# Batch 1's inverse stage in units of three y tiles, the ordering copies ahead of hswish, and one first-stage copy on VectorE

## The chip, the cores and the metric

The kernel runs on one core of a Trainium2 chip. The metric is device time in microseconds (us) of one execution. The engines are named as in the profile: PE (TensorE: matmuls, its weight loads in a row of their own, PEld), DVE (VectorE), ACT (ScalarE), POOL (GpSimd) and SP (SyncE, here only a queue that issues DMAs).

## What is computed

```python
def _attn_ref(x, filt_r, filt_i):            # x: (8, 3008, 256), filt: (1505, 256)
    X = np.fft.rfft(x, axis=1)
    Y = X * (filt_r + 1j * filt_i)[None]
    return np.fft.irfft(Y, n=x.shape[1], axis=1)

def _moe_ref(x, w_in, w_out):                # x: (24064, 256), w_in: (256, 2048), w_out: (2048, 256)
    h = x @ w_in
    g = h * np.clip(h + 3.0, 0.0, 6.0) / 6.0
    return g @ w_out
```

The second function takes the first one's output, all eight batches as 24064 tokens. All is in float32.

## The kernel before

**The second part sets the pace.** The 24064 tokens are 47 blocks of 512, and the 2048 hidden columns are 8 parts of 256. The loop at line 1190 goes through items i = 8k + p (block k, part p); one pass is called *step i* here. A step computes the up products of (k, p) and the down products of the item before it. Both are done with seven products in place of eight, so that there are sums to make around them: `t_sums` on POOL (line 760, per block), `g_sums` and `g_last` on DVE (821, 822, 827, per step). In a step PE does, in this order: `up_1` (three products of line 764), the work of *place 0*, `down` 1 (line 843), `up_2`, `down` 2 and 4, `up_3`, `down` 5 and 6, the work of *place 1*, `up_5`, `down` 7 and 3. What the vector side does for it:

- ACT copies products out of PSUM (775, 776, 785, 804) and computes two relus (809, called relu 0 and relu 1).
- DVE makes two sums from PSUM (790, 795) and two hswish products (814). hswish 0 is issued at line 1246 after relu 0; hswish 1 is issued at the head of the next step, in `g_sums`, and `down` 2 and 4 need it.
- At the first part of a block the last block's output is finished: `out_4` (918, 919) reads the PSUM bank that `down` 5 opens again, `out_5` (923) another; at the last part `out_1` (900), `out_2` (909) and `out_3` (914).

**The first part is threaded into these steps.** For each batch b from 1 on: a first stage (`a_unit` for batch 1, `a6_unit` for the others), a store to DRAM and a load back, a second stage (`b_unit`), the filter (`f_unit`, three DVE instructions 560 to 562, then `y_unit`, two DVE instructions 571 and 572, per y tile), an inverse stage, and a store to `g_tmp`, from where `t4_load` and `n_five`/`n_unit` (704, 715) take it, some steps later, and write `xn`. There are 12 y tiles per batch. The inverse stage is `bi_unit` for batches 0 and 1, two y tiles per unit, and `bi3_unit` for batches 2 to 7, three y tiles per unit.

- `bi_unit` (line 583): eight matmul passes into two PSUM banks of the pool psF, then two ACT copies (586); its store is two DMAs on the POOL queue (630).
- `bi3_unit` (line 599): 24 passes in three rounds, into two psF banks and the bank `be`. The bank `be` is written in round one and in round three, from different rows of PE. Between them stands the *ordering copy* (601): DVE copies two columns of `be` as soon as round one has written them, and round three waits for that. Then ACT copies one bank (602), DVE the rest of `be` (603, called the third copy), and ACT the other bank after relu 1 (610, in `bi3_copies`). Its store is four DMAs on the POOL queue (615, 618). `a6_unit` has the same ordering copy (483).

**What sets the order.** Everything is in program order on each engine. A table, `plan`, says in which step and place a unit is issued: place 0 for `a_unit`, `b_unit`, `bi_unit`, `n_five`, `n_unit`; place 1 for `w_scale`, `bi3_unit`, `a6_unit`; place 2, at the end of the step, for the rest (stores, loads, sums, `f_unit`, `y_unit`). `places(1)` gives the steps of batch 1: `a_unit` in steps 2 to 9, `b_unit` and `f_unit` in 12, 13, 15, 18, 19, 20, 22, 23, 26, 27, 28, 30, `y_unit` in 14, 15, 16, 19, 21, 22, 24, 25, 27, 29, 30, 31, `bi_unit` in 16, 21, 24, 29, 31, 32. For batches 2 to 7 `bi3_unit` falls on steps with p = 3 and p = 1, in turn. `late` (line 1186) moves `g_last` within a step, by p and by what the step before held. psF has two banks, the pools of `be` and of the tile t that a unit stores have one buffer each.

In place 0 of step 8 (block 1, p = 0) `a_unit` does chunk c = 6 of batch 1: ACT copies its first bank (456), and `a_sums` in place 2 lets DVE copy the second (464).

Of the kernel before, what the change touches and what calls it, by code (L numbers as in the profile page):

```python
# [12 lines left out]
AXT = mybir.ActivationFunctionType  # L13
# [26 lines left out]
NB = HC // XC  # L40
# [142 lines left out]
def kernel(  # L183
# [9 lines left out]
    nc = tc.nc  # L193
# [54 lines left out]
    st = {}  # L248
# [161 lines left out]
    def copy(dve, to, ps):  # L410
        if dve:
            nc.vector.tensor_copy(out=to, in_=ps)
        else:
            nc.scalar.activation(out=to, in_=ps, func=AXT.Copy)
# [22 lines left out]
    def bank(b):  # L437
        if b:
            return psF.tile([P, 512], FP32, name="psf", tag="f")
        st["bank"] = i = (st.get("bank", -1) + 1) % 4  # L440
        return psO.tile([P, 2, 2, P], FP32, name="po%d" % i).rearrange("p a u m -> p (a u m)")
# [4 lines left out]
    def a_unit(b, c):  # L446
        xc = xs[:, (b * NB + c) % 3, :, :]
        t = t1p.tile([P, XC // 2, 2, D], FP32, name="t1")
        ps = [bank(b).rearrange("p (j d) -> p j d", d=D) for h in range(2)]
        for j in range(2):  # L450
            for g in range(2):
                for h in range(2):
                    nc.tensor.matmul(ps[h][ts(g, 64), j, :], wa[ds(h * 64, NA), ds((c * XC + 2 * g + j) * 2 * KH, 64)],
                                     xc[ds(h * 64, NA), 2 * g + j, :], start=True, stop=True)
        for h in range(2 if b == 1 and c < NB - 2 else 1):
            nc.scalar.activation(out=t[:, :, h, :], in_=ps[h], func=AXT.Copy)
        st["t1", b, c] = t, ps[1]


# [129 lines left out]
    def bi3_unit(b, i):  # L589
        ys = [st.pop(("y", b, i + v)) for v in range(3)]  # L590
        c = psU.tile([P, 512], FP32, name="be")
        banks = [psF.tile([P, 512], FP32, name="psf", tag="f") for ri in range(2)]
        t = t3p.tile([P, 3, 2, D], FP32, name="t3")
        to = [t[:, q, :, :].rearrange("p u d -> p (u d)") for q in range(3)]
        for r in range(3):
            for v in range(2):
                for ri in range(2):
                    x, u, ps, o = (2, v, c, ri) if r == 2 * ri else (v, r - 1 + ri, banks[ri], r - 1 + ri)
                    nc.tensor.matmul(ps[ts(v, 64), ts(o, D)], wi[ts(ri, 64), 0, :], ys[x][ts(ri, 64), u, :], start=True, stop=True)  # L599
            if r == 0:  # L600
                nc.vector.tensor_copy(out=to[2][:, 0:2], in_=c[:, 0:2])
        nc.scalar.activation(out=to[1], in_=banks[1], func=AXT.Copy)
        nc.vector.tensor_copy(out=to[2][:, 2:512], in_=c[:, 2:512])
        st["t3", b, i] = t
        st["bi3"] = to[0], banks[0]

    def bi3_copies():
        if "bi3" in st:
            to, ps = st.pop("bi3")
            nc.scalar.activation(out=to, in_=ps, func=AXT.Copy)  # L610

    def g3_store(b, i):
        t = st.pop(("t3", b, i))
# [22 lines left out]
    for b in range(B):  # L636
# [4 lines left out]
        n = 0  # L641
# [170 lines left out]
    def hswish(k, p, i):  # L812
        o = (G11, G12)[i]
        nc.vector.scalar_tensor_tensor(out=st["g", k, p][:, o:o + 2, :].rearrange("p a n -> p (a n)"),  # L814
                                       in0=st["r", i], scalar=1.0, in1=st["h"][i], op0=ALU.min, op1=ALU.mult)
# [159 lines left out]
    def at(step, fn, *a):  # L975
        plan.setdefault((step, 0 if fn in EARLY else 1 if fn in (w_scale, bi3_unit, a6_unit) else 2), []).append((fn, a))

    with tc.manual_schedule():
# [43 lines left out]
        ps = psU.tile([P, 512], FP32, name="al")  # L1022
# [117 lines left out]
        def places(n):  # L1140
            if n == 1:
                return (list(range(2, NB + 2)), [12, 13, 15, 18, 19, 20, 22, 23, 26, 27, 28, 30],
                        [14, 15, 16, 19, 21, 22, 24, 25, 27, 29, 30, 31], [16, 21, 24, 29, 31, 32])
            k = first[n] * NP
            a_at = [k - 7 * NP + i for i in A_AT]
            f_at, y_at, bi_at = ([k - (5 - 2 * r) * NP + i for r in range(2) for i in p]
                                 for p in ((2, 3, 6, 7, 12, 13), (4, 5, 10, 11, 14, 15), (11, 17)))
            return a_at, f_at, y_at, bi_at
# [4 lines left out]
        for n in range(1, B):  # L1153
            a_at, f_at, y_at, bi_at = places(n)
            for c, s in enumerate(a_at):
                at(s, a_unit if n == 1 else a6_unit, n, c)
                at(s, a_sums if n == 1 else a6_sums, n, c)
                at(s, *((z_store, n, c, nc.sync) if n == 1 else (z6_store, n, c)))
                if c >= (3 if n == 1 else 2):
                    at(max(a_at[c - 3 + (n > 1)], s - 6), x_load, n, c)  # L1160
                elif n > 1:
                    at(max(prev[-1 if n == 2 else c - 2], s - 6), x_load, n, c)
            for c in range(NT):
                s = f_at[2 * (c - TB) + (n == 1)] + 1 if c >= TB else a_at[-1] + 1
                at(s, t2_load, n, c)
                s = f_at[2 * (c - FB) + 1] + 1 if c >= FB else a_at[-1 if n > 1 else 3] + 1
                at(s, table_load, n, c)
            for i in range(NU):
                if i % 2 == 0 or n == 1:
                    at(f_at[i], b_unit, n, i)  # L1170
                if n == 1 and i % 2 == 0:
                    at(bi_at[i // 2], bi_unit, n, i)
                    at(bi_at[i // 2], g_store, n, i)
                if n > 1 and i % 3 == 0:
                    at(bi_at[i // 3], bi3_unit, n, i)
                    at(bi_at[i // 3], g3_store, n, i)
                at(y_at[i], y_unit, n, i)
            for i in range(NU):
                at(f_at[i], f_unit, n, i)
            prev = a_at  # L1180

        HEAVY = (f_unit, y_unit, a_sums, n_five, a6_sums, bi3_unit)

        def late(i):
            return i % NP in (1, 2) or any(fn in HEAVY for place in range(3) for fn, a in plan.get((i - 1, place), ()))

        items = [(k, p) for k in range(NBLK) for p in range(NP)]
        for i in range(len(items) + 1):  # L1190
            up = i < len(items)
            k, p = items[min(i, len(items) - 1)]
            dn = i > 0
            kd, pd = items[i - 1]
            def do(place):
                for fn, a in plan.get((i, place), ()):
                    fn(*a)

            if k == 0:
                plain_up(p)  # L1200
                do(0)
                if dn:
                    plain_down(pd)
                do(1)
                do(2)
                continue
            if not up:
                last_down()
                break
            up_1(k, p)  # L1210
            ends = k == LAST and p == NP - 1
            do(0)
            last_plain = dn and kd == 0
            dn = dn and kd > 0
            if dn:
                g_sums(kd, pd)
                if not late(i):
                    g_last(kd, pd)
                down(kd, pd, 1)
            if up:  # L1220
                up_2(k, p)
            if dn and pd == 0 and kd > 1:
                out_4(kd - 1)
            if up:
                up_2b(k, p)
            if dn:
                down(kd, pd, 2, 4)
                if pd == NP - 1:
                    out_1(kd)
            if up:  # L1230
                up_3(k, p)
                if dn and late(i) and not (pd == 0 and kd > 1):
                    g_last(kd, pd)
            if dn:
                down(kd, pd, 5, 6)
            if up:
                up_4(k, p)
            if ends:
                out_1(k)
            if last_plain:  # L1240
                plain_down(pd, (0,))
            if dn and pd == 0 and kd > 1:
                out_5(kd - 1)
                g_last(kd, pd)
            if up:
                hswish(k, p, 0)
                do(1)
            if up:
                up_5(k, p)
            bi3_copies()  # L1250
            if last_plain:
                plain_down(pd, (1,))
                plain_out()
            if dn:
                if pd == NP - 1 or ends:
                    out_2(kd)
                down(kd, pd, 7, 3)
                if pd == NP - 1 or ends:
                    out_3(kd)
            do(2)  # L1260
# [30 lines left out]
```

## Time and profile before

Three runs of the kernel took 2650.63, 2651.26 and 2653.53 us, median 2651.26 us. The profiled execution took 2651.27 us, of which its span, from the first to the last instruction, is 2649.5 us.

| | busy us | share of the span |
|---|---|---|
| PE matmul | 2634.2 | 99% |
| PE weight load | 2338.2 | 88% |
| DVE | 2045.6 | 77% |
| ACT | 1299.8 | 49% |
| POOL | 484.2 | 18% |

The mean granted clock of PE is 1.00 from step 8 on. The timeline of the weight loads shows each step: its first load of line 764 from `xn` into `be` marks the start, and the next one of that kind the end. Times "at 2.17" below count from there. The lengths of steps by what else they hold (starts in the timeline subtracted from each other):

| step holds | steps | length, us |
|---|---|---|
| nothing more | 208 | 6.15 (one 6.98) |
| `b_unit` of batch 1 | 12 | 7.01; in 20, 23, 28: 7.36; in 26: 7.64 |
| `n_five` | 32 | 7.66 to 7.75 |
| one `n_unit` (four matmul passes) | 3 | 6.60 |
| `a6_unit` of three tiles | 18 | 7.88 |
| the same and `n_five` | 12 | 9.39 |
| `bi_unit` of batch 1, steps 16, 21, 24, 29, 31, 32 | 6 | 8.91, 7.69, 7.69, 7.70, 8.91, 7.37 |
| `bi3_unit`, p = 3 | 9 | 7.86 |
| `bi3_unit`, p = 3, and one `n_unit` (steps 267, 315) | 2 | 8.61 |
| `bi3_unit`, p = 3, and `n_five` (step 299) | 1 | 10.08 |
| `bi3_unit`, p = 1, steps 81, 129, 177, 225, 257, 273, 321 | 7 | 7.96 |
| `bi3_unit`, p = 1, steps 65, 113, 161, 209, 305 | 5 | 8.29 to 8.30 |

In a plain step (34, from 320.17 us) the loads of `down` 2 and 4 begin at 2.17, those of `down` 5 and 6 at 3.50, and DVE's hswish 0 ends at 5.27.

### The profile page before, as it was taken

To read this page: it belongs to the slowest core of one execution; us is meant where nothing else is said; L and a number is where in the kernel's file an instruction comes from. 1 tells how busy PE (TensorE), PEld (TensorE's weight loads), DVE (VectorE), ACT (ScalarE), POOL (GpSimd) and SP (SyncE) were. 2 spreads that over 40 slices of the span, in tenths; PEclk is the share of its full clock that TensorE was granted. 3 is DMA by queue.
4 is the path that set the end of the run, shared out by engine and by line. 5 is a ranking of instruction groups with operands and counts; after the bars stand their busy time and mean duration, and the time that the engine had idled before them with its cause. 6 is when DMAs were issued, how large, how long until landed. Compare 5 with 4: busy or idle time off the path is not lost.

```text
span 2649.5 us, 54856 instructions
## 1 busy us (share of the span) xinstructions
PE 2634.2 (99%) x21872; PEld 2338.2 (88%) x21872; DVE 2045.6 (77%) x3602; ACT 1299.8 (49%) x2682; POOL 484.2 (18%) x707
## 2 busy tenths in 40 slices
PE   9999999999999999999999999999999999999999
PEld 6688888989889898898988988889888888999998
DVE  7878767887678876788767887688877878766666
ACT  4554444444545445454444544545445454454554
POOL 2242022121211202111021210211112120111110
PEclk9999999999999999999999999999999999999999
DMA  9732234112241133411233112331223321110000
GB/s 245 222 94 70 71 84 116 54 32 81 77 119 52 32 84 80 113 52 36 81 86 107 52 37 80 89 103 52 55 61 89 103 56 48 48 43 22 19 21 25
DMA packets 130646, 198.29 MB, mean 75 GB/s; under 512 B 21538, under 2 KB 97408, under 8 KB 130198
## 3 DMA queue, kind: packets, MB, share of 16 engines
q1 hardware_dynamic: 115165, 150.12, 20.8%
q0 software_dynamic: 14656, 44.16, 6.0%
q8 instruction: 173, 2.83, 0.4%
q14 instruction: 83, 0.68, 0.1%
q10 hardware_dynamic: 569, 0.50, 0.1%
HBM read 122.43 MB, written 83.98 MB: 78 GB/s over the span
## 4 chain that ended last, share of the span: by engine, by line
PE 96%; DMA 2%; DVE 2%; issue 0%; SPq 0%; ACT 0%; POOL 0%; POOLq 0%; DVEq 0%
PE po L843 43%; PE al L764 24%; PE be L764 18%; PE psn L704 2%; PE psf L539 1%; PE psf L480 1%; PE po L886 1%; PE be L599 1%; PE psf L599 1%; PE psf L583 1%; PE be L480 1%; DVE g L814 0%; PE al L875 0%; PE be L875 0%; DMA ft<-in_filt_i_dram 0%; PE po L548 0%
## 5 line engine op out<-in xcount | busy, mean ns | idle before, releaser
L843 PEld LDWEIGHTS po<-w_all,g 128*128 128x128 f32 x10276 | 1369.6, 191 | 112.5 <-issue 20.3
L843 PE MATMUL po<-w_all,g 128*128 128x128 f32 x10276 | 1395.0, 276 | 1.1 <-DVE g L814 0.9
L809 ACT ACTIVATE r<-h,half_c 128x512 f32<-128x512 f32 x736 | 531.0, 721 | 336.0 <-DVE h L790 324.0
L764 PE MATMUL al<-xt,w_all 128*128 128x256 f32 x2208 | 659.6, 381 | 0.1
L814 DVE SCALAR_TENSOR_TENSOR g<-r,h 128x512 f32<-128x512 f32 x736 | 534.1, 727 | 151.9 <-ACT r L809 135.8
L764 PE MATMUL be<-xt,w_all 128*128 128x256 f32 x1472 | 437.8, 379 | 0.0
L790 DVE TENSOR_TENSOR h<-be,s 128x512 f32<-128x512 f32 x368 | 253.6, 689 | 153.0 <-PE be L764 144.5
L764 PEld LDWEIGHTS al<-xt,w_all 128*128 128x128 f32 x2208 | 335.4, 192 | 1.0 <-issue 0.5
L764 PEld LDWEIGHTS be<-xt,w_all 128*128 128x128 f32 x1472 | 279.7, 190 | 37.9
L760 POOL TENSOR_TENSOR xt<-xn 128x256 f32<-128x256 f32 x184 | 142.7, 795 | 874.1 <-ACT xn L686 840.3
L804 ACT ACTIVATE h<-al 128x256 f32<-128x256 f32 x368 | 141.4, 384 | 298.4 <-PE al L764 298.4
L795 DVE TENSOR_TENSOR h<-al,s 128x256 f32<-128x256 f32 x368 | 156.0, 424 | 156.7 <-PE al L764 156.1
L822 DVE TENSOR_TENSOR g<-g 128x512 f32<-128x512 f32 x367 | 261.3, 712 | 12.6
L785 ACT ACTIVATE s<-al 128x256 f32<-128x256 f32 x368 | 141.4, 384 | 212.1 <-PE al L764 210.6
L764 PE MATMUL al<-xn,w_all 128*128 128x256 f32 x736 | 226.0, 389 | 0.0
L776 ACT ACTIVATE s<-be 128x256 f32<-128x256 f32 x368 | 141.4, 384 | 171.7 <-PE be L764 171.7
L764 PE MATMUL be<-xn,w_all 128*128 128x256 f32 x736 | 218.9, 379 | 0.0
L821 DVE TENSOR_TENSOR g<-g 128x256 f32<-128x256 f32 x367 | 167.1, 455 | 12.6
L775 ACT ACTIVATE s<-al 128x256 f32<-128x256 f32 x368 | 141.2, 384 | 65.5 <-PE al L764 65.5
L827 DVE TENSOR_TENSOR g<-g 128x256 f32<-128x256 f32 x367 | 160.1, 436 | 2.5
L764 PEld LDWEIGHTS be<-xn,w_all 128*128 128x128 f32 x736 | 139.8, 190 | 18.9
L920 POOL TENSOR_TENSOR o<-p,o 128x256 f32<-128x256 f32 x46 | 36.7, 799 | 602.4 <-DVE o L918 557.1
(171 smaller groups left out, 1927.8 us busy)
## 6 DMA issues: line engine op xcount, KB each, us to landing
t<-g_tmp SPq DMA_DIRECT2D x184, 120.0 KB
t<-z_tmp SPq DMA_DIRECT2D x42, 512.0 KB
g_tmp<-t POOLq DMA_DIRECT2D x72, 256.0 KB, 5.7
z_tmp<-t POOLq DMA_DIRECT2D x120, 144.0 KB, 3.4
o_tmp<-o SPq DMA_DIRECT2D x46, 256.0 KB
xs<-in_x_dram SPq DMA_DIRECT2D x60, 192.0 KB
ft<-in_filt_r_dram SPq DMA_DIRECT2D x168, 64.0 KB
ft<-in_filt_i_dram SPq DMA_DIRECT2D x168, 64.0 KB
```

Source lines behind the costliest of these rows:

```text
L760: nc.gpsimd.tensor_tensor(out=o, in0=x0, in1=x1, op=op_)
L764: nc.tensor.matmul(ps, w_in[p][:, w, :], x, start=start, stop=stop, skip_group_check=True)
L776: nc.scalar.activation(out=s5, in_=be[:, 1, :], func=AXT.Copy)
L785: nc.scalar.activation(out=s[:, 1, :], in_=al, func=AXT.Copy)
L790: nc.vector.tensor_tensor(out=st["h"][0].rearrange("p (a n) -> p a n", a=2), in0=be, in1=s, op=ALU.add)
L795: nc.vector.tensor_tensor(out=st["h"][1][:, 256:512], in0=al, in1=s5, op=ALU.add)
L809: nc.scalar.activation(out=r, in_=st["h"][i], func=AXT.Relu, bias=half_c, scale=1.0 / 6.0)
L814: nc.vector.scalar_tensor_tensor(out=st["g", k, p][:, o:o + 2, :].rearrange("p a n -> p (a n)"), in0=st["r", i], scalar=1.0, in1=st["h"][i ...
L821: v.tensor_tensor(out=g[:, G1, :], in0=g[:, G3, :], in1=g[:, G22, :], op=ALU.add)
L822: v.tensor_tensor(out=g[:, G3:G2 + 1:2, :], in0=g[:, G3:G1 + 1, :], in1=g[:, G11:G11 + 1, :].broadcast_to([P, 2, 256]), op=ALU.subtract)
L827: nc.vector.tensor_tensor(out=g[:, G4, :], in0=g[:, G12, :], in1=g[:, G2, :], op=ALU.subtract)
L843: nc.tensor.matmul(st["po", k][bank][:, part, u, :], g[:, a, ts(u, P)], w_out[p][:, w, :], start=(p == 0 and n in OPENS and u == 0), stop= ...
```

## The change

- Batch 1's inverse stage is issued as four `bi3_unit`s with `g3_store`, in place 1 of steps 17, 24, 29 and 32, instead of six `bi_unit`s with `g_store` in place 0 of steps 16, 21, 24, 29, 31 and 32. The y tile of step 25 is issued in step 24.
- Place 1 of a step comes ahead of hswish 0, so that on DVE the ordering copies (601, 483) stand before it. The third copy (603) goes to `bi3_copies`, and so stays behind hswish 0 on DVE. ACT's and PE's orders are not touched by this part.
- In `a_unit`, chunk c = 6 of batch 1 (step 8): the first bank's copy is DVE's instead of ACT's.

```diff
@@ a_unit
         for h in range(2 if b == 1 and c < NB - 2 else 1):
-            nc.scalar.activation(out=t[:, :, h, :], in_=ps[h], func=AXT.Copy)
+            copy(c == NB - 2, t[:, :, h, :], ps[h])
@@ bi3_unit
         nc.scalar.activation(out=to[1], in_=banks[1], func=AXT.Copy)
-        nc.vector.tensor_copy(out=to[2][:, 2:512], in_=c[:, 2:512])
         st["t3", b, i] = t
-        st["bi3"] = to[0], banks[0]
+        st["bi3"] = to[0], banks[0], to[2], c
 
     def bi3_copies():
         if "bi3" in st:
-            to, ps = st.pop("bi3")
+            to, ps, third, c = st.pop("bi3")
             nc.scalar.activation(out=to, in_=ps, func=AXT.Copy)
+            nc.vector.tensor_copy(out=third[:, 2:512], in_=c[:, 2:512])
@@ places
             if n == 1:
                 return (list(range(2, NB + 2)), [12, 13, 15, 18, 19, 20, 22, 23, 26, 27, 28, 30],
-                        [14, 15, 16, 19, 21, 22, 24, 25, 27, 29, 30, 31], [16, 21, 24, 29, 31, 32])
+                        [14, 15, 16, 19, 21, 22, 24, 24, 27, 29, 30, 31], [17, 24, 29, 32])
@@ the plan
                 if i % 2 == 0 or n == 1:
                     at(f_at[i], b_unit, n, i)
-                if n == 1 and i % 2 == 0:
-                    at(bi_at[i // 2], bi_unit, n, i)
-                    at(bi_at[i // 2], g_store, n, i)
-                if n > 1 and i % 3 == 0:
+                if i % 3 == 0:
                     at(bi_at[i // 3], bi3_unit, n, i)
                     at(bi_at[i // 3], g3_store, n, i)
                 at(y_at[i], y_unit, n, i)
@@ the loop over items
             if up:
+                do(1)
                 hswish(k, p, 0)
-                do(1)
             if up:
                 up_5(k, p)
             bi3_copies()
```

`copy(True, to, ps)` is a DVE `tensor_copy`, `copy(False, to, ps)` an ACT copy.

## The prediction

> **What bounds the kernel.** The page first: busy times, the chain that ended last, and the wait of a vector copy that will matter.
>
> ```profile
> span 2649.5 us, 54856 instructions
> PE 2634.2 (99%) x21872; PEld 2338.2 (88%) x21872; DVE 2045.6 (77%) x3602; ACT 1299.8 (49%) x2682; POOL 484.2 (18%) x707
> PE 96%; DMA 2%; DVE 2%; issue 0%; SPq 0%; ACT 0%; POOL 0%; POOLq 0%; DVEq 0%
> L603 DVE COPY t<-be 128x510 f32<-128x510 f32 x24 | 16.5, 689 | 18.4 <-PE be L599 18.4
> ```
>
> PE sets the end. Only two things shorten the kernel: fewer or better packed PE passes, and fewer steps in which PE waits for DVE. A plain step is 6.15 us 207 times of 208, so I price every touched step by its excess over its own work. PE's work for one `bi_unit` is 7.37 − 6.15 = 1.22 us (step 32, the one that nothing holds up); for one `bi3_unit` 7.86 − 6.15 = 1.71 (nine steps); `b_unit` 0.86 (7.01 − 6.15), `n_five` 1.51.
>
> Next the timeline, where bi3 units meet a slow DVE. First DVE, then the weight loads, of step 299:
>
> ```profile
> 2145.39 0.82 DVE L827 TENSOR_TENSOR g<-g 128x256 f32<-128x256 f32 x1
> 2146.13 1.21 DVE L814 SCALAR_TENSOR_TENSOR g<-r,h 128x512 f32<-128x512 f32 x1
> 2147.27 0.15 DVE L601 COPY t<-be 128x2 f32<-128x2 f32 x1
> 2148.18 0.69 DVE L603 COPY t<-be 128x510 f32<-128x510 f32 x1 [0.77 <-PE be L599]
> ```
>
> ```profile
> 2145.83 0.13 PEld L599 LDWEIGHTS be<-y,wi 64*64 64x64 f32 x1
> 2147.46 0.13 PEld L599 LDWEIGHTS be<-y,wi 64*64 64x64 f32 x1 [0.59 <-DVE t L601]
> ```
>
> Round three waits for the ordering copy, and the copy stands behind hswish 0 (814). The same in a bi3 step without trouble (59):
>
> ```profile
> 496.88 0.68 DVE L814 SCALAR_TENSOR_TENSOR g<-r,h 128x512 f32<-128x512 f32 x1
> 496.99 0.13 PEld L599 LDWEIGHTS be<-y,wi 64*64 64x64 f32 x1
> 497.70 0.16 DVE L601 COPY t<-be 128x2 f32<-128x2 f32 x1
> ```
>
> There the copy runs 0.71 after the unit's first load (497.70 − 496.99), 0.14 after hswish 0: round one was the last to end. In step 299 it runs 1.44 after (2147.27 − 2145.83). Last, batch 1's region: step 16's loads, then DVE and one load of steps 25 and 26.
>
> ```profile
> 186.71 0.19 PEld L583 LDWEIGHTS psf<-y,wi 64*64 64x64 f32 x4 [0.33 <-issue]
> 188.26 0.20 PEld L583 LDWEIGHTS psf<-y,wi 64*64 64x64 f32 x4 [1.36 <-DVE s L562]
> 189.27 0.52 PEld L843 LDWEIGHTS po<-w_all,g 128*128 128x128 f32 x4 [0.81 <-issue]
> ```
>
> ```profile
> 253.75 0.69 DVE L571 TENSOR_TENSOR y<-s 64x512 f32<-64x512 f32 x1
> 255.27 0.69 DVE L814 SCALAR_TENSOR_TENSOR g<-r,h 128x512 f32<-128x512 f32 x1
> 257.40 0.41 DVE L919 TENSOR_TENSOR o<-po,o 128x256 f32<-128x256 f32 x1
> 260.12 1.21 DVE L814 SCALAR_TENSOR_TENSOR g<-r,h 128x512 f32<-128x512 f32 x1
> 261.37 1.10 DVE L571 TENSOR_TENSOR y<-s 64x512 f32<-64x512 f32 x1
> 264.80 0.97 PEld L843 LDWEIGHTS po<-w_all,g 128*128 128x128 f32 x8 [0.77 <-DVE g L814]
> ```
>
> `bi_unit` in step 16 needs a psF bank that the filter still reads; `down` 2 in step 26 waits for hswish 1, behind a y tile that took 1.10 us per instruction while POOL made sums.
>
> **Part 1, the ordering copy ahead of hswish 0 (batches 2 to 7).** Nothing is added; two DVE instructions trade places. What each bi3 step loses now is the copy's distance from the unit's first load, less 0.71:
> - step 299: 1.44 − 0.71 = 0.73; its length agrees: 10.08 − (7.66 + 1.71) = 0.71.
> - steps 267 and 315: 8.61 − (6.60 + 1.71) = 0.30 each, 0.60.
> - steps 65, 113, 161, 209, 305: copy at 0.97 (5.86 − 4.89), 0.26 late. Of 8.30 − 7.86 = 0.44 I take 0.25; the other 0.19 is a wait for `out_4` (919) and stays. 1.25 in all.
> - the seven of 7.96: 0.10 each, 0.70.
> - nine of 7.86: nothing.
>
> After the change the copy has only `g_last` or `out_5` ahead of it, done by 6.59 in step 299 where the copy can start at 6.20 + 0.71 = 6.91, and by 5.34 against 5.60 in step 65. So the whole 0.71 + 0.60 + 1.25 + 0.70 = **−3.26 us**.
>
> The price is a later hswish 0: 0.14 + 0.16 us of waiting and copying in step 59, up to 1.3 us in an `a6_unit` step. What covers it: in step 59 it would end at 5.57 + 0.69 = 6.26, and the third copy waits for PE until 6.34. In the 30 `a6_unit` steps (36: copy ends 5.59, so hswish 0 at 6.28) the next DVE instruction (495) waits for ACT until 6.77 anyway. Queued behind on DVE are the sums 495 to 498 and hswish 1 of the next step, which ends at 1.69 there with PE's load due at 2.17: 0.48 us of cover more. Without any cover the cost would be 0.69 × 30 = 21 us at most; I take 0. A bi3 step also needs its t buffer free ahead of the copy; the stores landed long before.
>
> **Part 2, batch 1 in four units.** PE work 6 × 1.22 = 7.32 becomes 4 × 1.71 = 6.84, so −0.48. ACT loses 12 copies of 0.60 (586) and gets 8; DVE gets four ordering copies (0.15) and four third copies (0.69), 3.4 us more. POOL issues 16 DMAs (0.60 and 0.68, lines 615 and 618) for 12 (0.60, line 630); no SP transfer moves. The last store is now issued in step 33, by 317, and lands 5.7 us later, near 323; `t4_load` of batch 1 comes in step 36, from 332.9. The stores of step 24 pass POOL at 1.0 to 3.3 of step 25, as in step 66, ahead of block 4's sums, which start at 3.70 there already.
>
> The rest is waits, worked out step by step from DVE's order. A rule from step 20: hswish 1 ended at 3.42, the load of `down` 2 came at 3.47 instead of 2.17 + 0.86 = 3.03, and the step was 0.35 longer; so PE loses the lateness less 0.09.
> - 16: no unit. DVE is as before until hswish 1 ends at 3.40; load at 3.45 for 2.17, 1.28 − 0.09: 6.15 + 1.19 = 7.34 (8.91 before).
> - 17: 7.66 + 1.71 = 9.37 (7.71). The copy waits only for `g_last`, slow beside POOL, ending 6.89, and is due at 6.92.
> - 21: filter to 1.46, hswish 1 to 2.18, load 2.23 for 2.17: 6.20 (7.69).
> - 24: 6.15 + 1.71 and 0.04: 7.90 (7.69). 29 alike: 7.90 (7.70).
> - 25: y tiles 6 and 7 both run at its head, 0.47 to 3.32; hswish 1 to 4.11, load 4.16 for 3.68. Beside POOL's sums 821 and 822 take 0.83 and 1.09 (rows of step 18), to 6.09; 918 and 919, which read PSUM and are not slowed, to 6.83. `down` 5 opens the bank that 919 reads: 6.88 for 5.01, 1.78 lost, and 0.2 for `g_last` behind: 7.66 + 1.98 = 9.64 (7.74). Without slowing by POOL 919 ends at 5.90 and the step is 8.46; with hswish 1 slowed too (1.21, step 299's row) 919 ends at 7.35, and it is 10.2. I take 9.64, since the rows of step 18 have just this overlap.
> - 26: one y tile fewer at its head, 7.01 (7.64).
> - 31: as 16, 7.34 (8.91). 32: 6.15 + 1.71 = 7.86 (7.37).
>
> Sum after 70.56, before 71.36: **−0.8 us**, between −2.0 (step 25 at 8.46) and −0.1 (10.2, and 24, 29 at 7.96 as other bi3 steps).
>
> Two pages of the Trainium skill bear on this. "SBUF — State Buffer", SBUF: two separate sides, has DVE instructions with two SBUF inputs and GpSimd lock each other out for a whole instruction; this trace's 1.21 for 0.69 agrees in kind, and by the rule in full, with each DVE instruction behind a whole POOL sum, step 25 would be near 10.2. "Perfetto Trace Analysis", Optimizing Scalar/DVE Operations, advises offloading from DVE to Scalar where DVE is saturated, and speaks against this change; here DVE is 77% busy over all and its extra copies fall into waits for PE, so by the rule part 2 would cost time, and by the rows it gains a little.
>
> **Part 3, the copy in step 8.** ACT gives up 0.60 at 2.36 to 2.96; the next ACT copy (785, at 2.93) waits for PE, its usual 0.74 after the load of `up_2` (2.19). DVE is idle from 1.54 to 3.43 there and takes 0.68 (464). 0 both ways; without that idle time 790 would be up to 0.68 late.
>
> **Sum.** −3.26 − 0.8 + 0 = −4.1. The profiled execution took 2651.27 us (span 2649.5 and 1.8 around it), beside a median of 2651.26, so no correction: **2647.2 us**, −0.15%. Its own range: −5.3 to −2.7, that is 2646.0 to 2648.6.
>
> **Rivals.**
> - *Both terms at the good end:* POOL's sums don't meet step 25 (part 2 at −2.0), part 1 in full, and 0.02 from each of the 30 `a6_unit` steps, whose loads show waits for 483. −5.9: 2645.4. For it: 9.2 us of such waits. Against: DVE was idle ahead of 27 of those 30 copies, so an earlier place brings nothing.
> - *The swap does nothing:* the copy stays late behind `out_5` and `g_last`. Only part 2 is left: 2650.5. Against: 5.34 to 5.60 in step 65.
> - *Slower, DVE held at the ordering copy:* it is the first to write t, of which there is one buffer, so it waits for the store before it to land; now hswish 0 waits with it, and so PE's next step. Places: 18 of the 30 `a6_unit`s stand two steps behind another. Issue at 342.45 takes 2.03, landing 3.4 (the page), done at 347.9; the next copy runs at 353.9. It decides from 6 us later landings on; held 0.6 us each, 18 × 0.6 − 4.1 = +6.7: 2658. No DVE wait for a store shows in the waits.
>
> **How the numbers follow.** 0.2%, 5.3 us, is about what a measurement of this kernel can tell from no change. Forecast 0.64 (within it), good end 0.22 (faster), no swap 0.07 (within), slower 0.07. So faster 0.22, same 0.71, slower 0.07. The range adds to the forecast's own the good end in part, the second rival, and the runs' spread (−0.6 to +2.3 about their median): 2645.0 to 2650.4.
>
> **What would show it.** Right: 299 near 9.4, 65 near 8.05, the 7.96 steps at 7.86; 601 ahead of 814 with no load waiting for it; 16 and 31 near 7.34; the longest wait in batch 1 in step 25, for 919. Wrong: `a6_unit` steps over 7.88 or the next ones over 6.15 (hswish 0 is late); step 25 under 8.5 or over 10.2; steps after 36 of other lengths without a bi3 unit.

## The result, and the profile after

The changed kernel takes 2647.17 us (median of 20 runs, 2645.85 to 2648.53), the kernel before 2651.19 us (20 runs, 2650.51 to 2653.53). The ratio is 0.9983, with a 95% interval from 0.9977 to 0.9990. The head of the page after, and the row of the copy that was at line 603 and is now at 610:

```profile
span 2646.4 us, 54959 instructions
PE 2628.5 (99%) x21920; PEld 2338.1 (88%) x21920; DVE 2051.1 (78%) x3611; ACT 1296.5 (49%) x2677; POOL 486.6 (18%) x711
PE 97%; DVE 2%; DMA 1%; issue 0%; ACT 0%; SPq 0%; POOL 0%; POOLq 0%; DVEq 0%
L610 DVE COPY t<-be 128x510 f32<-128x510 f32 x28 | 19.3, 688 | 4.2 <-PE be L599 4.1
```

DVE got 5.5 us more work and PE's busy time fell by 5.7 us. The third copy hardly waits for PE any more (4.2 us over 28 copies, 18.4 over 24 before): hswish 0 now fills that time. The profiled execution took 2648.2 us. Its span fell by 3.1 us only, because its step 8 began 1.28 us later (128.88 for 127.60 us): the start, where PE waits for the load of x, lasted from 126.3 to 128.9 us in the ten profiled executions of this study, whatever the kernel. So parts are compared by lengths of steps, which repeat to 0.02 us, and not by spans.

Of 368 steps 24 changed by more than 0.02 us. Before and after, in us:

| step | before | predicted | after | change |
|---|---|---|---|---|
| 16 | 8.91 | 7.34 | 7.36 | −1.55 |
| 17 | 7.71 | 9.37 | 9.40 | +1.68 |
| 21 | 7.69 | 6.20 | 6.15 | −1.54 |
| 24 | 7.69 | 7.90 | 7.86 | +0.17 |
| 25 | 7.74 | 9.64 | 9.37 | +1.64 |
| 26 | 7.64 | 7.01 | 7.01 | −0.63 |
| 29 | 7.70 | 7.90 | 7.86 | +0.16 |
| 31 | 8.91 | 7.34 | 7.36 | −1.55 |
| 32 | 7.37 | 7.86 | 7.86 | +0.49 |
| *batch 1 together* | 71.36 | 70.56 | 70.23 | −1.13 |
| 81, 129, 177, 225, 257, 273, 321 | 7.96 | 7.86 | 7.86 | −0.71 |
| 65, 113, 161, 209, 305 | 8.29 to 8.30 | 8.05 | 8.05 | −1.22 |
| 267, 315 | 8.61 | 8.31 | 8.30, 8.31 | −0.61 |
| 299 | 10.08 | 9.37 | 9.37 | −0.71 |
| *batches 2 to 7 together* | | −3.26 | | −3.24 |

Where a row has several steps, the change is their sum. Over all steps it is −4.37. The medians differ by 4.02.

Step 299 shows the first half of it. DVE's timeline, then the two loads into `be` that matter (start, duration, engine, line, instruction; in brackets the idle time before it and what ended it):

```profile
2143.65 0.82 DVE L827 TENSOR_TENSOR g<-g 128x256 f32<-128x256 f32 x1
2144.81 0.16 DVE L601 COPY t<-be 128x2 f32<-128x2 f32 x1 [0.33 <-PE be L599]
2144.88 0.72 DVE L814 SCALAR_TENSOR_TENSOR g<-r,h 128x512 f32<-128x512 f32 x1
2145.73 0.69 DVE L610 COPY t<-be 128x510 f32<-128x510 f32 x1
```

```profile
2144.09 0.13 PEld L599 LDWEIGHTS be<-y,wi 64*64 64x64 f32 x1
2145.02 0.13 PEld L599 LDWEIGHTS be<-y,wi 64*64 64x64 f32 x1
```

The ordering copy now runs 0.72 after the unit's first load, and the wait goes the other way: DVE waits for PE's round one. Round three follows 0.93 after the first load, 1.63 before. Step 25 shows what the second half gave back, again DVE, then POOL's sums, then the weight loads:

```profile
255.92 0.69 DVE L572 TENSOR_TENSOR y<-s 64x512 f32<-64x512 f32 x1
256.71 0.69 DVE L814 SCALAR_TENSOR_TENSOR g<-r,h 128x512 f32<-128x512 f32 x1
257.44 0.83 DVE L821 TENSOR_TENSOR g<-g 128x256 f32<-128x256 f32 x1
258.31 1.10 DVE L822 TENSOR_TENSOR g<-g 128x512 f32<-128x512 f32 x1
259.66 0.41 DVE L919 TENSOR_TENSOR o<-po,o 128x256 f32<-128x256 f32 x1
```

```profile
257.03 2.95 POOL L760 TENSOR_TENSOR xt<-xn 128x256 f32<-128x256 f32 x3 [0.40 <-ACT xn L686]
```

```profile
257.46 0.97 PEld L843 LDWEIGHTS po<-w_all,g 128*128 128x128 f32 x8 [0.47 <-DVE g L814]
260.12 0.97 PEld L843 LDWEIGHTS po<-w_all,g 128*128 128x128 f32 x8 [1.47 <-DVE o L919]
```

The second y tile ends at 256.61. Then 821 and 822, with both inputs in SBUF, take 0.83 and 1.10 instead of 0.42 and 0.69 while POOL makes block 4's sums (three of them in the row shown), and `down` 5 waits 1.47 us for 919, which comes after them.

### The profile page after: what moved, and what is told of

The parts are those of the page before. It is cut to its first block, busy times and chain, and to the rows that moved or that the text cites. A ratio compares the mean times of both kernels' runs of the same rounds, so it can differ in the third digit from the quotient of the medians.

```text
span 2646.4 us, 54959 instructions
## 1 busy us (share of the span) xinstructions
PE 2628.5 (99%) x21920; PEld 2338.1 (88%) x21920; DVE 2051.1 (78%) x3611; ACT 1296.5 (49%) x2677; POOL 486.6 (18%) x711
## 4 chain that ended last, share of the span: by engine, by line
PE 97%; DVE 2%; DMA 1%; issue 0%; ACT 0%; SPq 0%; POOL 0%; POOLq 0%; DVEq 0%
PE po L843 43%; PE al L764 24%; PE be L764 18%; PE psn L704 2%; PE psf L539 1%; PE psf L480 1%; PE po L886 1%; PE psf L599 1%; PE be L599 1%; PE be L480 1%; DMA w_all<-in_x_dram 1%; PE al L875 0%; PE be L875 0%; PE po L548 0%; DVE g L814 0%
```

## The experiments

Each is compared with its own runs of the kernel before, and step by step with the kernel that it was made from. The question was which of the three parts gives what, whether they add, and whether the reasons given for the waits are the real ones.

**The swap alone.** The kernel before with only this (and the third copy moved to `bi3_copies`):

```diff
             if up:
+                do(1)
                 hswish(k, p, 0)
-                do(1)
```

> Only the swap: place 1 ahead of hswish 0, the third copy behind it; batch 1 and step 8 as before. Theory (the ordering copy's lateness behind hswish 0 is what the 15 bi3 steps lose): 3.25 us shorter than before, near 2648.0, with steps 65, 113, 161, 209, 305 at 8.05, the seven of 7.96 at 7.86, 267 and 315 at 8.30, 299 at 9.37, and no other step changed. Rival A (all of the gain is batch 1's fewer units): 0. Rival B (a late hswish 0 costs something in the 30 a6 steps that hides a larger gain): a6 steps over 7.88 or 9.39, or the steps after them over their 6.15.

Measured: 2647.94 us, ratio 0.9988 (0.9979 to 0.9997). The fifteen steps named changed, to 8.04 or 8.05, 7.86, 8.30 or 8.31 and 9.36, −3.24 us in sum, and no other step by more than 0.02 us; the `a6_unit` steps kept their 7.88 and 9.39. Rivals A and B fall.

**Batch 1's units alone.** The changed kernel with `hswish` ahead of `do(1)` again and the copy of step 8 on ACT.

> Only batch 1's four units of three, with the y tile of step 25 in step 24; place 1 stays behind hswish 0, the copy of step 8 stays with ACT. Theory: the units alone bring nothing, because step 17's ordering copy then stands behind a hswish 0 that POOL's sums slow to 1.2 us: the copy 1.2 late, step 17 near 10.55 instead of 9.40, 24 and 29 some 0.05 longer; with the other steps as in the changed kernel (-1.1 in all) the sum is +0.1, near 2651.3. Rival A (the units are the gain): 1.1 to 4 us shorter.

Measured: 2651.78 us, ratio 1.0002 (0.9993 to 1.0011); the steps sum to +0.15. Steps 16, 21, 25, 26, 31 and 32 are as in the changed kernel, 24 and 29 are 7.92 for 7.86, and step 17 is 10.53 for 9.40. Its hswish 0, ordering copy and the load that waits for it:

```profile
200.98 1.21 DVE L814 SCALAR_TENSOR_TENSOR g<-r,h 128x512 f32<-128x512 f32 x1
202.11 0.15 DVE L601 COPY t<-be 128x2 f32<-128x2 f32 x1
```

```profile
202.31 0.13 PEld L599 LDWEIGHTS be<-y,wi 64*64 64x64 f32 x1 [1.04 <-DVE t L601]
```

So the parts don't add: −3.24 and +0.15 make −3.09, the whole is −4.37. The units of three are worth their place only with the swap, which saves 1.13 in step 17 and 0.06 to 0.07 in each of 24 and 29 besides its 3.24.

**The copy of step 8 alone.**

```diff
-            nc.scalar.activation(out=t[:, :, h, :], in_=ps[h], func=AXT.Copy)
+            copy(c == NB - 2, t[:, :, h, :], ps[h])
```

> Only the copy of step 8 on VectorE. Theory: DVE is idle when it comes and ACT's next copy waits for PE either way: no step changes, 0 us. Rival (ACT was the late one in blocks 0 and 1): step 8 under 8.07, up to 0.6 us.

Measured: 2650.92 us, ratio 0.9998 (0.9989 to 1.0007). No step changed; step 8 is 8.07 as before. The copy stands in idle time of DVE, as the timeline shows:

```profile
129.34 0.69 DVE L412 COPY t<-psf 128x512 f32<-128x512 f32 x1 [0.77 <-PE psf L453]
130.46 0.69 DVE L790 TENSOR_TENSOR h<-be,s 128x512 f32<-128x512 f32 x1 [0.42 <-PE be L764]
```

**The eighth y tile back in step 25.** The changed kernel with

```diff
-                        [14, 15, 16, 19, 21, 22, 24, 24, 27, 29, 30, 31], [17, 24, 29, 32])
+                        [14, 15, 16, 19, 21, 22, 24, 25, 27, 29, 30, 31], [17, 24, 29, 32])
```

> The changed kernel with the eighth y tile back in step 25. Theory (two y tiles at the head of step 25 push 821, 822 into POOL's sums and 919 behind them): step 25 back to 7.7 from 9.37, step 26 back to 7.64 from 7.01, 1.0 us shorter than the changed kernel, near 2646.1. Rival (step 25 is long because the store's DMA issues and the third copy of step 24 come before it): step 25 stays over 9, and 26 gets longer: 0.6 us longer than the changed kernel.

Measured: 2646.25 us, ratio to before 0.9982 (0.9973 to 0.9991). Against the changed kernel step 25 is 7.71 for 9.37 and step 26 7.64 for 7.01, together −1.03, and nothing else moved. The y tile's move to step 24 is the one part of the change that lost time.

**POOL's sums kept out of step 25's head.** The changed kernel, with block 4's sums issued at the end of step 25, so that on POOL they stand behind the addition of line 920, which waits for 918:

```diff
-        if (t + n) // PAIRS > t // PAIRS > 0:
+        if (t + n) // PAIRS > t // PAIRS > 0 and t // PAIRS != 4:
...
         at(LAST * NP + 3, b12_back)
+        at(25, t_sums, 4)
```

> The changed kernel, with POOL's sums for block 4 issued at the end of step 25 instead of by its n_five, so that on POOL they stand behind 920, which waits for 918. Theory (of the 1.64 us that step 25 got longer, the second y tile alone makes some 0.8, and POOL's sums, which slow 821 and 822, the rest): 821 and 822 back to 0.42 and 0.69 us in step 25, the load behind 919 at 5.95 instead of 6.79, step 25 near 8.55 for 9.37; step 26, where the sums now run beside hswish 1, 821 and 822, up to 0.1 longer; 0.75 us shorter than the changed kernel, near 2646.4. Rival (the y tile alone: the sums don't matter): step 25 stays at 9.37.

Measured: step 25 is 8.88 for 9.37, −0.49, and no other step changed. The time, 2647.19 us (ratio to before 0.9984, 0.9975 to 0.9993), can't tell half a us. DVE and two weight loads of step 25:

```profile
257.39 0.43 DVE L821 TENSOR_TENSOR g<-g 128x256 f32<-128x256 f32 x1
257.85 0.69 DVE L822 TENSOR_TENSOR g<-g 128x512 f32<-128x512 f32 x1
260.38 0.96 DVE L827 TENSOR_TENSOR g<-g 128x256 f32<-128x256 f32 x1
```

```profile
259.26 0.97 PEld L843 LDWEIGHTS po<-w_all,g 128*128 128x128 f32 x8 [0.66 <-DVE o L919]
261.39 0.52 PEld L843 LDWEIGHTS po<-w_all,g 128*128 128x128 f32 x4 [0.26 <-DVE g L827]
```

821 and 822 are back to 0.43 and 0.69, and the load behind 919 comes at 5.98 of the step, where 5.95 was expected: the slowing is POOL's sums. The step was expected at 8.55 and is 0.33 longer. Of that, 0.26 is what I had left out: the sums then ran beside `g_last` (827, 0.96 for 0.41), and the last down product waited for it (the last row).

**Three y tiles moved earlier.** The changed kernel with

```diff
-                        [14, 15, 16, 19, 21, 22, 24, 24, 27, 29, 30, 31], [17, 24, 29, 32])
+                        [14, 14, 16, 19, 21, 21, 24, 25, 27, 29, 29, 31], [17, 24, 29, 32])
```

> The changed kernel with the y tiles in steps 14, 14, 16, 19, 21, 21, 24, 25, 27, 29, 29, 31, that is, the second, sixth and eleventh one step earlier and the eighth one step later. Theory (PE waits where y tile and filter of one step stand ahead of hswish 1 in a step without b_unit; two y tiles alone fit): 16 and 31 from 7.36 to 6.15, 23 from 7.36 to 7.01, 25 to 7.71, 26 to 7.64, no other step changed: -1.21 - 1.21 - 0.35 - 1.04 = 3.8 us shorter than the changed kernel, near 2643.4, 7.8 shorter than before. Rival (DVE's load is what counts, not its order): the waits move to the steps beside and the time stays within 1 us of 2646.2.

Measured: 2643.23 us, ratio to before 0.9970 (0.9959 to 0.9982). Against the changed kernel 16 and 31 are 6.15 for 7.36, 23 is 7.01 for 7.36, 25 is 7.72 for 9.37, 26 is 7.64 for 7.01, 17 is 9.37 for 9.40: −3.79 in sum. DVE has the same instructions and the waits did not move elsewhere. This version beats both kernels: the slowest of its seven runs, 2644.07 us, is under the fastest of the changed kernel, 2645.85.

**One and two more instructions ahead of hswish 0.** The changed kernel with a useless addition behind the ordering copy of each `a6_unit` of three tiles; once, and in a second kernel twice:

```diff
                 nc.vector.tensor_copy(out=t[:, 2, 1, 0:2], in_=be[:, D:D + 2])
+                for _ in range(1):
+                    nc.vector.tensor_tensor(out=spare, in0=wai[:, 0:512], in1=wai[:, 512:1024], op=ALU.add)
```

> The changed kernel with one more VectorE instruction (an addition of two constant 128x512 tiles into a spare tile, some 0.69 us, its result unused) between the ordering copy and hswish 0 in each of the 30 a6 units of three tiles. Theory (a later hswish 0 is covered: 0.59 us until 495 and 0.48 us more until the next step's load for hswish 1): hswish 0 ends near 6.87 for 6.18, 495 comes 0.1 late, steps of 7.88 and the 6.15 after them keep their length; up to 2 us in all from the few of 9.39 where POOL's sums slow VectorE: 2647 to 2649. Rival (hswish 0 is on the path): 0.7 us in each of 30, 21 us longer, near 2668.

> The same with two such instructions. Theory: 1.4 us later is more than the cover of 1.07; 495 0.8 late, hswish 1 of the next step ends near 2.5, its load comes near 2.55 instead of 2.17, the step after each a6 unit 0.3 longer, the a6 steps themselves unchanged: 8 to 10 us longer than the changed kernel, near 2656. Rival (no such limit): no longer than with one, or 42 us.

Measured: with one, 2651.80 us (ratio to before 0.9999, 0.9989 to 1.0009), +5.2 us by steps against the changed kernel; with two, 2672.57 us (1.0082, 1.0064 to 1.0100), +26.6 by steps. With one, the 18 plain `a6_unit` steps kept 7.88, as the theory had it; the 12 with `n_five` went from 9.39 to between 9.74 and 10.00; in these hswish 0 runs beside POOL's sums and now takes 1.21 or 1.22. With two, the 18 became 8.42 and the 12 between 10.88 and 11.14, and the step after each 0.11 shorter. Both expectations were too low, and not by the size alone: the wait is in the `a6_unit` step's end, not in the next step. Step 36 in the changed kernel, DVE and the first load of step 37 into `be`:

```profile
338.57 0.68 DVE L814 SCALAR_TENSOR_TENSOR g<-r,h 128x512 f32<-128x512 f32 x1
340.29 0.42 DVE L496 TENSOR_TENSOR t<-be,t 128x256 f32<-128x256 f32 x1
```

```profile
340.95 0.41 PEld L764 LDWEIGHTS be<-xn,w_all 128*128 128x128 f32 x2
```

The same with two more (line numbers are larger by three: 817 is hswish, 498 and 499 are 495 and 496):

```profile
337.32 0.68 DVE L817 SCALAR_TENSOR_TENSOR g<-r,h 128x512 f32<-128x512 f32 x1
337.92 0.41 DVE L498 TENSOR_TENSOR t<-be,t 128x256 f32<-128x256 f32 x1
338.37 0.42 DVE L499 TENSOR_TENSOR t<-be,t 128x256 f32<-128x256 f32 x1
```

```profile
338.91 0.30 PEld L767 LDWEIGHTS be<-xn,w_all 128*128 128x128 f32 x2 [0.56 <-PE al L767]
```

496 is the last reader of the bank `be`, and the next step's first product into `be` loads 0.12 after its end (338.79 to 338.91). The row names a PE product as what ended the wait, but in all 42 steps that got longer, 12 with one more and 30 with two, the load stands 0.12 after 496, to 0.002 us. In the changed kernel it stands 0.23 after 496 in step 36 (7.65 and 7.88 of the step), so 0.11 was free there, behind the 0.59 between the end of hswish 0 and 495, which waits for ACT. With two more, hswish 0 ends 1.33 later (7.51 for 6.18) and the step is 0.54 longer. So a late hswish 0 is covered for 0.79 us and not for 1.07: 0.59, 0.11, and some 0.08 by which 495 starts before hswish 0 ends (337.92 and 338.00). Where POOL slows hswish 0 already, 0.53 is left: in step 44 it ends 1.14 later with one more (9.09 for 7.95) and the step is 0.61 longer.

## Why the prediction was right

- **The bound and the method.** PE sets the end, so the sum of step lengths is the time. That gave 2647.2 for a measured 2647.17. Part of that is luck: batch 1 came out 0.33 better than forecast in the steps, and the medians moved 0.35 less than the steps.
- **Part 1, −3.26.** Measured −3.24, step by step as listed, and shown to be the swap's alone. Each bi3 step lost the ordering copy's lateness, one for one, whether 0.10 or 0.71; in step 17, without the swap, it is 1.13. The 0.19 for `out_4` in the five steps stayed, as said: they are at 8.05.
- **Part 1's price of 0.** Right in value: no `a6_unit` step changed. Wrong in one reason: the second cover, 0.48 until the next step's load for hswish 1, is not what comes next; the bank `be` is, and the whole cover is 0.79. The first cover of 0.49 (0.59 after the change) was enough. The working named what is queued behind on DVE, but not who waits for 495 and 496 to free a bank.
- **Part 2, −0.8.** Measured −1.13. Eight of nine steps lie within 0.05. Step 25 was 0.27 shorter than forecast: 919's end was 0.10 early, and the 0.2 for `g_last` did not come, since PE was late enough. That both the y tile and POOL's sums make this step long was shown by taking each away. What the prediction didn't say is that part 2 depends on part 1: its 9.37 for step 17 used the swap, and without it the units bring nothing (+0.15). Two of its figures don't follow from its rows: by its rule 919's end at 5.90 gives 8.51 for step 25 and not 8.46, and the ends of its parts add up to −5.3 and −3.4, so that for −2.7 as the upper end of its own range no sum is shown. The measured time lies inside either way.
- **Part 3, 0.** Measured 0, for the reason given.
- **The rivals.** "Good end" falls: no time came from the `a6_unit` loads' waits for 483; DVE now waits ahead of all 30 of those copies. "No swap" falls by the first experiment. "DVE held at the ordering copy" did not occur: all its waits there are for PE (14.7 us ahead of 601, 30.7 ahead of 483). A landing that comes too late was not tried.
- **The two pages.** The Trainium skill, "SBUF — State Buffer" (SBUF: two separate sides), says that of a DVE instruction with two SBUF inputs and a GpSimd one, whichever starts first holds the shared ports for its whole instruction while the other waits. The prediction made of it a whole POOL sum ahead of each DVE instruction, and 10.2 for step 25. The rows show less, 0.40 and 0.41 more for 821 and 822, where a sum alone takes 0.73, and step 25 at 9.37. But a DVE instruction that starts inside a sum has, by the page, only the rest of that sum to wait for, and 821 started at 4.10 of the step, inside the sum from 3.70 to 4.66. So the rows speak against the prediction's reading; on the page's rule they don't decide, since that sum took longer too, 0.96. Its "Perfetto Trace Analysis" (Optimizing Scalar/DVE Operations) says that offloading work from DVE to Scalar may make sense where DVE is saturated. The prediction read that as speaking against the change, but DVE, busy 78% of the time, is not saturated here. The copies that moved from ACT to DVE cost nothing: step 8 kept its length, and steps 24, 29 and 32 are at the 7.86 that PE's work takes.

## What to carry to other kernels

Where one engine is full and repeats a pattern, subtract the pattern's length from each pass and explain the excess: that prices an edit to a tenth of a us where runs scatter by two. A tiny copy that a full engine waits for belongs ahead of every long instruction in its queue whose result is not yet due; before moving it, list for each instruction that becomes late which bank or buffer it frees, and who takes that next. The work of an engine that is not full costs by where it stands: the same DVE instructions, ordered so that no two kinds of burst share a step without slack, took 3.8 us less.

## What the runs showed that I had not expected

- In the step after a wait PE's loads ran 0.11 us ahead: every step behind a lengthened `a6_unit` step was 6.04 for 6.15 or 6.83 for 6.94. So 0.1 of such a wait is made good, as with the 0.09 of the prediction's rule.
- DVE instructions that read PSUM (790, 795, 918, 919, the copies) were not slowed beside POOL's sums (0.41 and 0.69 with and without), those with two inputs in SBUF were: in the rows shown by 0.40 and 0.41 us (821, 822 in step 25), 0.52 (814, 1.21 for 0.69) and 0.55 (827, 0.96 for 0.41).
- The first 128 us, before the steps, differ by 2.6 us between executions of nearly the same instructions, more than half of what this change is worth.
